# Attention with a routed expert layer on one core: half of a block's second layer in the next expert's code, the hint first, and h transposed ahead of layer 1

## The chip, the cores and the metric

The kernel runs on 1 core of one Trainium2 chip. The metric is device time in microseconds (us). Before the change three runs gave 288.33, 290.68 and 290.84 us, the median is 290.68 us.

## The reference

The reference computes causal attention (2 batches, 8 heads, 576 positions, head size 64) mixed with a memory read-out, and sends its 1152 rows of 512 numbers through a layer of 8 experts. A row goes to the expert with the largest gate logit. An expert keeps at most 288 rows.

```python
logits = x @ w_gate;  expert_idx = np.argmax(logits, axis=1)      # 8 experts
disp[e, counts[e]] = x[i]                                         # rows of an expert, in order
h = np.maximum(np.einsum('ecd,edf->ecf', disp, w1), 0.0)          # layer 1: 512 -> 1024
y = np.einsum('ecf,efd->ecd', h, w2)                              # layer 2: 1024 -> 512
out[i] = gate_w[i] * y[expert_idx[i], pos[i]]
```

With the inputs used the experts are wanted by 12, 149, 0, 58, 1, 558, 9 and 365 rows.

## The kernel before

The first half of the kernel (attention, gate, routing) is laid out by a planner, the class `Steps`: each step has costs and due times, and the planner writes the instructions in the order in which its model runs them. It also hands out buffers of each kind, such as the softmax buffers "p". The second half is written in a fixed order, and it is where the change lies.

An expert's rows are cut into a first block of 32 rows, and up to two further blocks of 128. The count of further blocks, `cr[e]`, is 0, 1 or 2; here it is 0, 1, 0, 1, 0, 2, 0, 2 for the experts 0 to 7. It is read from memory into registers at run time (`counts_in`), and TensorE, VectorE, ScalarE and GpSimd branch on it.

The loop at line 1117 writes one stretch of code for each expert e. In order:

- a branch hint for TensorE (line 1118), which names the branch `rest{e}` and carries whether `cr[e] > 0`;
- `first_g1(e + 1)` (L799): layer 1 of the next expert's first block, and its relu to h on ScalarE (L800). For expert 0 it stands ahead of the loop, and so ahead of the hint;
- `first_turn(e)`: two transposes of h (L805), copied to hT by VectorE (L806);
- `first_g2(e)` (L814): layer 2 of the first block from hT, a scaling on VectorE (L816), and a scatter to the output on GpSimd (L753);
- `rest(e)`: a branch (L917) on `cr[e] > 0`, and inside it one branch for exactly one further block (`one`, L918) and one for two (`two`, L921). Where `cr[e]` is 0 the engines jump over both;
- `more_rows(e + 2)` (L715): GpSimd gathers the rows of the further blocks of expert e + 2;
- `paced(e + 4)` (L689, L703): SyncE loads the weights of expert e + 4.

`one` transposes the gathered rows (L749), copies them by ScalarE (L846), runs layer 1 (L851), splits h and the weights w2 into a rounded part and its rest (`split`, L824 on ScalarE and L825 on VectorE; four buffers of each in rotation), and runs layer 2 as 8 x 3 matmuls into one bank (L858). `put` scales the result (L833) and scatters it. `two` does the same for 256 rows with all of layer 1 split (L887), and layer 2 as 8 x 3 x 2 matmuls (L895), of which those with the rests are issued as two halves of 256 columns. Its block 1 is complete first, and block 2 still has its last 12 matmuls to do behind that.

Ahead of the loop stand, for the last two token tiles, `late_rows` (L771), which adds their rows to the first blocks by a selection matmul. The first blocks lie in two groups of four experts, g = 0 and 1; `upright(g)` (L761, L763) transposes what was gathered early, and `first_x(g)` copies the result for layer 1.

## Time and profile before

| | us |
|---|---|
| median of three runs | 290.68 |
| the profiled execution's own time | 289.64 |
| its span, first to last instruction | 287.9 |
| TensorE busy | 250.7 (87% of the span) |
| VectorE, ScalarE, GpSimd busy | 175.2, 138.2, 71.5 |

The span is time between the first and last instruction of the program; 1.74 us of the execution's time lie around it. A busy share is a mean over stages: up to about 142 us the attention runs, from there to the end the experts. A row of the list in order of time gives start, length, engine, line, operation, and in brackets the idle time of the engine just before it with what ended that. PEq and DVEq stand for the sequencers of TensorE and VectorE, at branches above all.

### The profile page before, as it was taken

How to read it: one execution, taken by the hardware profiler on the slowest of the kernel's cores; microseconds unless marked ns; L12 is line 12 of the kernel's file. 1: busy time of each engine (PE TensorE's matmuls, PEld its weight loads, DVE VectorE, ACT ScalarE, POOL GpSimd, SP SyncE). 2: the span in 40 equal slices, each digit the busy share in tenths (PEclk: the TensorE clock that was granted, in tenths of full speed). 3: DMA queues.
4: the chain of work that ended last, by engine and by line, in shares of the span. 5: the costliest groups of instructions: out<-in, count | busy, mean ns of one | idle time of the engine just before them, and what ended most of it. 6: DMA issues, size and time to landing. Idle time of an engine off the chain costs nothing.

```text
span 287.9 us, 6958 instructions
## 1 busy us (share of the span) xinstructions
PE 250.7 (87%) x2545; PEld 201.4 (70%) x2545; DVE 175.2 (61%) x461; ACT 138.2 (48%) x400; POOL 71.5 (25%) x87
## 2 busy tenths in 40 slices
PE   8989998989879999999993798489977999769992
PEld 6676776677667678878862496358745999549991
DVE  2998899976999989768520136112713873138731
ACT  4779876886867787640310134004403652026520
POOL 2413274352573502223011100301051000520002
PEclk9999999999999999999999899979999999999999
DMA  6969887969899499352246773868688770410001
GB/s 193 387 213 341 286 300 221 369 264 323 282 296 323 115 283 374 96 237 79 86 142 197 237 227 137 278 235 255 209 245 275 225 219 6 120 48 0 2 0 74
DMA packets 23955, 58.97 MB, mean 205 GB/s; under 512 B 2636, under 2 KB 9296, under 8 KB 23906
## 3 DMA queue, kind: packets, MB, share of 16 engines
q1 hardware_dynamic: 22530, 54.60, 57.0%
q0 software_dynamic: 1376, 3.75, 4.0%
q8 instruction: 27, 0.44, 0.6%
q14 instruction: 22, 0.18, 0.2%
HBM read 51.96 MB, written 6.82 MB: 204 GB/s over the span
## 4 chain that ended last, share of the span: by engine, by line
DMA 37%; issue 22%; PE 22%; DVE 11%; POOL 4%; ACT 2%; POOLq 1%; SPq 0%; ACTq 0%; DVEq 0%
DMA xe<-x_scr,igf 16%; DMA out<-ys,isc 9%; PE ps L344 5%; DMA q<-qk 4%; DMA out<-yo,isc 4%; PE ps L365 3%; DMA xg<-x_scr,ig 3%; PE ps L380 2%; PE ps L332 2%; PE ps L333 2%; PE ps L469 2%; PE ps L405 2%; PE ps L477 2%; DMA w<-qk 1%; DVE phi L974 1%
## 5 line engine op out<-in xcount | busy, mean ns | idle before, releaser
L340 ACT ACTIVATE p<-ps,nmx 128x128 f32<-128x128 f32 (+3 forms) x64 | 33.8, 533 | 7.0 <-DVE nmx L337 6.0
L825 DVE TENSOR_TENSOR lr<-w,hr 128x512 fp32r<-128x512 f32 x40 | 26.7, 689 | 6.8 <-ACT hr L824 4.8
L337 DVE TENSOR_REDUCE nmx<-ps 128x1 f32<-128x128 f32 (+3 forms) x64 | 29.3, 479 | 1.6 <-PE ps L334 0.7
L344 PE MATMUL ps<-cs,p 128*128 128x128 f32 x160 | 28.4, 285 | 1.4 <-ACT pT L252 0.9
L824 ACT CAST hr<-w 128x512 fp32r<-128x512 f32 x40 | 23.9, 618 | 9.0 <-PE ps L895 5.4
L252 ACT COPY pT<-ps 128x256 f32<-128x256 f32 (+4 forms) x62 | 24.1, 414 | 5.0 <-PE ps L344 2.5
L800 ACT ACTIVATE h<-ps 128x256 f32<-128x256 f32 x8 | 3.1, 383 | 48.2 <-PE ps L799 36.5
L753 POOL DMA_INDIRECT out<-yo,isc x6 | 5.9, 982 | 76.9 <-DVE yo L833 49.1
L799 PE MATMUL ps<-w,xf 128*32 128x256 f32 x192 | 14.1, 446 | 9.4 <-PEq L917 8.6
L814 PE MATMUL ps<-w,hT 128*32 128x128 f32 x512 | 16.7, 274 | 5.7 <-DVE hT L806 5.0
L344 PEld LDWEIGHTS ps<-cs,p 128*128 128x128 f32 x160 | 17.6, 141 | 5.6 <-ACT p L340 1.7
L365 PE MATMUL ps<-pT,v 128*64 128x256 f32 (+1 forms) x144 | 20.6, 352 | 0.0
L814 PEld LDWEIGHTS ps<-w,hT 128*32 128x32 f32 x512 | 13.8, 110 | 8.5 <-DVE hT L806 7.1
L806 DVE COPY hT<-ps 128x256 f32<-128x256 f32 x8 | 3.4, 425 | 26.3 <-PE ps L805 26.3
L829 DVE SCALAR_TENSOR_TENSOR hl<-ps,hh 128x256 fp32r<-128x256 f32 (+1 forms) x20 | 9.5, 477 | 15.8 <-ACT hh L828 15.7
L457 DVE TENSOR_TENSOR x<-ps,tmp 128x288 f32<-128x288 f32 (+2 forms) x37 | 16.0, 442 | 2.4 <-PE ps L477 2.0
L828 ACT ACTIVATE hh<-ps 128x256 fp32r<-128x256 f32 (+1 forms) x20 | 8.5, 426 | 18.4 <-PE ps L851 9.7
L753 POOL DMA_INDIRECT out<-ys,isc x8 | 8.0, 1002 | 37.0 <-DVE ys L816 26.4
L533 POOL TENSOR_TENSOR xr<-x 128x512 f32<-128x512 f32 (+1 forms) x8 | 10.3, 1284 | 27.4 <-DVE x L457 14.9
L799 PEld LDWEIGHTS ps<-w,xf 128*32 128x32 f32 x192 | 6.7, 125 | 14.8 <-issue 12.7
L279 POOL TENSOR_SCALAR q<-q 64x640 f32<-64x640 f32 (+1 forms) x14 | 11.7, 848 | 20.7 <-DMA q<-qk 20.4
L365 PEld LDWEIGHTS ps<-pT,v 128*64 128x64 f32 x144 | 12.3, 136 | 5.5 <-issue 0.7
(203 smaller groups left out, 665.8 us busy)
## 6 DMA issues: line engine op xcount, KB each, us to landing
w<-w SPq DMA_DIRECT2D x56, 512.0 KB
w0s<-w SPq DMA_DIRECT2D x8, 512.0 KB
q<-qk SPq DMA_DIRECT2D x7, 576.0 KB
kt<-qk SPq DMA_DIRECT2D x7, 576.0 KB
v<-v SPq DMA_DIRECT2D x8, 320.0 KB
phi<-qp SPq DMA_DIRECT2D x8, 288.0 KB
out<-zer SPq DMA_DIRECT2D x4, 576.0 KB
x_scr<-xr SPq DMA_DIRECT2D x8, 256.5 KB
```

The lines of the kernel that those rows point to most:

```text
L252: nc.scalar.copy(out=o, in_=i_)
L279: en(e).tensor_scalar(out=i_[64:128], in0=i_[64:128], scalar1=SCALE, scalar2=1.0, op0=ALU.mult, op1=ALU.mult)
L337: nc.vector.tensor_reduce(out=nm[:, j:j + 1], in_=Z[Sk][:, :w], axis=AX.X, op=ALU.max, negate=True)
L340: nc.scalar.activation(out=Z[pk][:, :w], in_=Z[Sk][:, :w], func=AF.Exp, bias=nm[:, j:j + 1], accum_out=sums[:, t, 2 * p + j:2 * p + j + 1])
L344: nc.tensor.transpose(Z[Tk][:, 128 * kb:128 * kb + 128], Z[pk][:, 128 * kb:128 * kb + 128], ident)
L365: nc.tensor.matmul(Z[M][64 * j:64 * j + 64, c:128 * mg], vt[n % 2][:, kb, 64 * j:64 * j + 64], Z["pT", n, gi, j][:, 128 * mg * kb + c:128 ...
L457: nc.vector.tensor_tensor(out=xa[:R, a:c, :], in0=m()[:, :, 0:LC], in1=bc(r, R, c - a, LC), op=ALU.mult)
L753: s = nc.gpsimd.indirect_dma_start(out=out if k else out0, out_offset=bass.IndirectOffsetOnAxis(ap=isc[:, cc:cc + 1], axis=0), in_=yo, in_ ...
L799: nc.tensor.matmul(ps[g * W0:(g + 1) * W0, 0:FG], xT[:, c, e * W0:(e + 1) * W0], a[:, c, g * FG:(g + 1) * FG], start=(c == 0), stop=(c == 3))
L814: nc.tensor.matmul(ps[y * W0:(y + 1) * W0, 0:DG], hT[:, 128 * r + g * W0:128 * r + (g + 1) * W0], c2[:, g * nr + r, y * DG:(y + 1) * DG], ...
L824: nc.scalar.copy(out=hv, in_=wv)
L825: return hv, lv, lambda: nc.vector.tensor_tensor(out=lv, in0=wv, in1=hv.bitcast(F32), op=ALU.subtract)
```

## The change

- `one` stops after the first 12 of its 24 layer 2 matmuls. The other 12 and `put` become a function `last(e)`, which stands in the next expert's stretch, right behind its hint, under a condition of its own. `two` does all of block 2 first and the first 12 matmuls of block 1, and leaves the other 12 of block 1 to `last(e)`. For expert 7 `last` stays inside `rest`.
- Some matmuls are issued as two halves of 256 columns, by a count for each expert (`FILL`), which sets how many instructions a stretch has. The warm-up at the start has 50 matmuls of 152 columns in place of 30 of 256.
- In each stretch `first_turn(e)` stands ahead of `first_g1(e + 1)`. In expert 0's stretch the hint stands ahead of `first_g1(1)`, and `upright(1)`, `late_rows(1)` and `first_x(1)` follow `first_turn(0)`.
- `more_rows(e + 2)` moves into the next stretch, behind `last(e)`.
- In `one`, the copy of the transposed rows is shared between ScalarE and VectorE.
- The buffers that `late_rows` reads (one "p" buffer, now fixed for this use, and the two "xr") move to the pool that stays open to the end; the counts are read ahead of `first_g1(0)`.

```diff
-HALF = 8
+FILL = ((34, 0), (34, 8), (34, 8), (34, 8), (34, 8), (34, 8), (34, 8), (0, 0))
...
+                for k in self.fixed.keys() & st[x][4] - self.at.keys():
+                    t0 = max([t0, *(b[0] for b in self.kinds[k[0]] if b[1] == self.fixed[k])] if any(b[1] == self.fixed[k] for b in self.kinds[k[0]]) else [float("inf")])
...
-    Z.buffers("p", [ap.tile([128, 512], F32, name=f"p{x}") for x in range(P["np"])])
+    Z.buffers("p", [(ap if x < P["np"] - 1 else const).tile([128, 512], F32, name=f"p{x}") for x in range(P["np"])])
+    Z.fixed["p", "pick"] = P["np"] - 1
...
-    Z.buffers("xr", [ap.tile([128, XW], F32, name=f"xr{x}") for x in range(2)])
+    Z.buffers("xr", [const.tile([128, XW], F32, name=f"xr{x}") for x in range(2)])
...
         x_t(e, 1, mps[3])
-        nc.scalar.copy(out=xT.rearrange("p c r -> p (c r)"), in_=mps[3])
+        i_ = mps[3].rearrange("p (c r) -> p c r", c=4)
+        nc.scalar.copy(out=xT[:, 0:2], in_=i_[:, 0:2])
+        nc.vector.tensor_copy(xT[:, 2:4], i_[:, 2:4])
...
-        for f in range(8):
+        for f in range(4):
             for y, (u, v) in enumerate(((hh, 0), (hl, 0), (hh, 1))):
-                nc.tensor.matmul(mps[2], u[:, f, 0:128], w[f][v], start=(f == 0 and y == 0), stop=(f == 7 and y == 2))
+                n = 2 if 3 * f + y > 11 - FILL[e][1] else 1
+                for z in range(n):
+                    c = slice(DM // n * z, DM // n * (z + 1))
+                    nc.tensor.matmul(mps[2][:, c], u[:, f, 0:128], w[f][v][:, c], start=(f == 0 and y == 0), stop=False)
             take()
+
+    def last(e):
+
+        hh, hl = mt_["hh"], mt_["hl"]
+        for f in range(4, 8):
+            hv, lv = mt_["hr"][f % 4], mt_["lr"][f % 4]
+            for y, (u, v) in enumerate(((hh, hv), (hl, hv), (hh, lv))):
+                nc.tensor.matmul(mps[2], u[:, f, 0:128], v, start=False, stop=(f == 7 and y == 2))
         put(e, 1, mps[2])
...
+        left = [FILL[e][0]]
+
         def g2(f, k):
...
-                n = 2 if f < HALF and i else 1
+                n = 2 if (f or i) and left[0] > 0 else 1
+                left[0] -= n - 1
...
-            g2(f, 1)
+            g2(f, 2)
             if f < 4:
-                g2(f, 2)
-        put(e, 1, mps[2])
-        for f in range(4, 8):
-            g2(f, 2)
+                g2(f, 1)
         put(e, 2, mps[3])
...
             with tc.If(cr[e] > 1, label=f"two{e}"):
                 two(e)
+            if e == E - 1:
+                last(e)
...
-        Z.add({"P": (213 * P["wu"][0], 0, 13, 107)}, lambda e: warm(P["wu"][0] + 8), ["zer"], [], -9e9)
+        Z.add({"P": (213 * P["wu"][0], 0, 13, 107)}, lambda e: warm(P["wu"][0] + 28, 152), ["zer"], [], -9e9)
...
         late_rows(0)
-        for g in range(1, NF):
-            upright(g)
-            late_rows(g)
         late_probs(fps)
...
-        for g in range(NF):
-            first_x(g)
+        first_x(0)
+        cr.extend(counts_in(ET.PE, ET.DVE, ET.Activation, ET.Pool))
         first_g1(0)
...
-        first_g1(1)
-        cr.extend(counts_in(ET.PE, ET.DVE, ET.Activation, ET.Pool))
         for e in range(E):
             tc.mark_branch_hint_location(f"rest{e}", hint=cr[e] > 0, engines=[ET.PE])
-            if 1 <= e < E - 1:
+            if e == 0:
+                first_g1(1)
+            else:
+                with tc.If(cr[e - 1] > 0):
+                    last(e - 1)
+                if e - 1 + LK < E:
+                    more_tiles(e - 1 + LK)
+                    more_rows(e - 1 + LK)
+            first_turn(e)
+            if e == 0:
+                for g in range(1, NF):
+                    upright(g)
+                    late_rows(g)
+                    first_x(g)
+            elif e < E - 1:
                 first_g1(e + 1)
-            first_turn(e)
             first_g2(e)
             rest(e)
-            if e + LK < E:
-                more_tiles(e + LK)
-                more_rows(e + LK)
             if e + 4 < E:
                 paced(e + 4)
```

## Rows read from the trace of the kernel before

**Rows 1.** The page's first part: busy time, share of the span, instructions.

```profile
PE 250.7 (87%) x2545; PEld 201.4 (70%) x2545; DVE 175.2 (61%) x461; ACT 138.2 (48%) x400; POOL 71.5 (25%) x87
```

**Rows 2.** TensorE in order of time: expert stretches 1 to 7.

```profile
157.70 3.31 PE L799 MATMUL ps<-w,xf 128*32 128x256 f32 x32 [4.34 <-PEq L917]
...
187.31 3.19 PE L799 MATMUL ps<-w,xf 128*32 128x256 f32 x32 [3.46 <-PEq L917]
...
208.84 1.93 PE L799 MATMUL ps<-w,xf 128*32 128x256 f32 x32 [0.73 <-PEq L921]
...
211.66 1.84 PE L814 MATMUL ps<-w,hT 128*32 128x128 f32 x49 [0.52 <-DVE hT L806]
213.82 0.68 PE L814 MATMUL ps<-w,hT 128*32 128x128 f32 x15 [0.33 <-issue]
215.36 1.93 PE L799 MATMUL ps<-w,xf 128*32 128x256 f32 x32 [0.85 <-PEq L917]
...
218.18 1.96 PE L814 MATMUL ps<-w,hT 128*32 128x128 f32 x64 [0.52 <-DVE hT L806]
...
249.80 1.39 PE L814 MATMUL ps<-w,hT 128*32 128x128 f32 x38 [1.42 <-DVE hT L806]
251.53 1.05 PE L814 MATMUL ps<-w,hT 128*32 128x128 f32 x26 [0.34 <-issue]
253.05 0.43 PE L805 MATMUL ps<-cs,h 128*128 128x128 f32 x2 [0.47 <-PEq L917]
```

**Rows 3.** Stretches: us, busy (instructions) by engine, granted clock, DMA share, GB/s.

```profile
157.70:163.80 6.10, 5.58 (x98) 3.32 (x98) 0.42 (x1) 0.38 (x1) 0.00 (x0) 0.77 0.64 201
...
187.30:193.70 6.40, 5.76 (x98) 3.38 (x98) 0.47 (x2) 0.38 (x1) 0.00 (x0) 0.73 0.71 238
208.20:214.60 6.40, 4.83 (x98) 3.00 (x98) 1.17 (x3) 0.38 (x1) 3.04 (x3) 1.00 0.82 228
```

**Rows 4.** TensorE in order of time: expert 1's single block.

```profile
164.10 0.63 PE L749 MATMUL ps<-cs,xg 128*128 128x128 f32 x4 [0.25 <-issue]
165.44 7.41 PE L851 MATMUL ps<-x,w 128*128 128x128 f32 x64 [0.72 <-ACT x L846]
172.61 0.47 PE L858 MATMUL ps<-hr,hh 128*128 128x512 f32 x1
...
177.95 0.39 PE L858 MATMUL ps<-lr,hh 128*128 128x512 f32 x1
179.08 1.93 PE L799 MATMUL ps<-w0s,xf 128*32 128x256 f32 x32 [0.74 <-PEq L921]
```

**Rows 5.** In order of time, TensorE and VectorE: the second group's late rows.

```profile
142.37 0.39 PE L761 MATMUL ps<-zer 128*128 128x512 bf16 x1
...
145.55 1.31 PE L777 MATMUL ps<-xr,p 128*128 128x1 f32 x8
...
142.87 0.42 DVE L783 COPY xf<-ps 128x256 f32<-128x256 f32 x1 [2.26 <-ACT xf L782]
```

**Rows 6.** GpSimd and TensorE in order of time; last row: gathered tile's landings.

```profile
212.33 1.02 POOL L715 DMA_INDIRECT xg<-x_scr,ig  x1 [0.31 <-issue]
...
249.86 1.02 POOL L715 DMA_INDIRECT xg<-x_scr,ig  x1 [0.31 <-issue]
...
220.92 1.07 PE L749 MATMUL ps<-cs,xg 128*128 128x128 f32 x8 [0.79 <-DVEq L918]
...
257.03 1.09 PE L749 MATMUL ps<-cs,xg 128*128 128x128 f32 x8 [1.08 <-DVEq L918]
...
DMA to landing us min/median/max: 6.0/6.1/6.3
```

**Rows 7.** TensorE in order of time: layer 2 of expert 5's two blocks.

```profile
234.61 0.40 PE L895 MATMUL ps<-hr,hh 128*128 128x512 f32 x1
...
245.75 0.40 PE L895 MATMUL ps<-lr,hh 128*128 128x256 f32 x2
```

**Rows 8.** SyncE's queue in order of time: expert 6's first weights, fourth piece landed.

```profile
206.71 0.24 SPq L703 DMA_DIRECT2D seen<-w  x1
```

More of the change, by code (lines that the diff above doesn't have):

```diff
@@ L48, in __init__ @@
         self.steps, self.writer, self.readers, self.kinds, self.at = [], {}, {}, {}, {}
+        self.fixed = {}
     def buffers(self, kind, tiles):
@@ L118, in emit @@
                 if k not in self.at:
-                    b = min(self.kinds[k[0]])
+                    b = min(b for b in self.kinds[k[0]] if b[1] == self.fixed.get(k, b[1]))
                     self.kinds[k[0]].remove(b)
@@ L891, in g2 @@
             for i, (a, v) in enumerate(((hh, hv), (hl, hv), (hh, lv))):
-                n = 2 if f < HALF and i else 1
+                n = 2 if (f or i) and left[0] > 0 else 1
+                left[0] -= n - 1
                 for y in range(n):
                     c = slice(DM // n * y, DM // n * (y + 1))
-                    nc.tensor.matmul(mps[1 + k][:, c], a[:, f, 128 * k - 128:128 * k], v[:, c], start=(f == 0 and i == 0), stop=(f == 7 and i == 2 and y == n - 1))
+                    nc.tensor.matmul(mps[1 + k][:, c], a[:, f, 128 * k - 128:128 * k], v[:, c], start=(f == 0 and i == 0), stop=(k == 2 and f == 7 and i == 2 and y == n - 1))
         for f in range(2):
```

## Prediction

> **What bounds the kernel now.** I read the first part of the page first: TensorE is busy 87% of the span, no other engine over 61% [rows 1]. So what TensorE does not do in the expert part is what can be won, and I went through that part in TensorE's order of time and wrote down every idle time. Three kinds recur. The first is the jump over an expert without further blocks, put down to TensorE's own sequencer: 4.34 us ahead of stretch 1, 3.46 ahead of 3, but only 0.85 ahead of 5 and 0.47 ahead of 7 [rows 2]. The second stands behind the transposes of h in every stretch: 0.52 us until VectorE has copied hT, 1.42 in stretch 6 [rows 2]. The third is 0.73 or 0.74 us behind a single block [rows 2, 4]. The table by stretches adds that the two long jumps cost twice: in the stretch behind them the granted clock is 0.77 and 0.73, elsewhere 1.00 [rows 3], and the first layer 1 there takes 3.31 and 3.19 us in place of 1.93 [rows 2]. [...] Idle times of 0.85 and 1.42 us lowered nothing that shows.
>
> Why two jumps are cheap and two dear: the hint stands at the head of a stretch (for expert 0 behind its layer 1), so I took the time from there to the jump. In stretch 4 it is 5.67 us (208.84 to 215.36 less 0.85), in 2 it is 4.77 (179.08 to 187.31 less 3.46), in 6 about 6.5 (from 246.1, where the last row of layer 2 ends, to 253.05 less 0.47) [rows 2, 4, 7]. In 0 it is about 2.9, worked out as the 5.67 less its layer 1 (1.93) and less 0.88, by which its layer 2 is longer than the usual 1.96 (211.66 to 214.50, with a pause of 0.33) [rows 2]. From hint to the next work that makes 7.2, 8.2, 6.5 and 7.0 us. **I read it so:** what the hint starts takes 5.7 us or more, and the jump waits for what is left. In both stretches with a cheap jump layer 2 has that pause and takes 0.82 to 0.88 us more (stretch 6: 249.80 to 252.58); I count it as a price of a hint that takes effect.
>
> **The change part by part.** All against the profiled execution, 289.64 us.
>
> The jumps. In stretches 2, 4 and 6 the change puts the last 12 matmuls of the block between hint and jump. Layer 2 of a single block goes at 0.232 us per matmul (172.61 to 177.95, 23 steps) [rows 4], so that is 2.8 us, and with transposes and layer 1 (208.84 to 211.66 less 0.52: 2.30) and layer 2 (1.96) the hint has 7.1 us [rows 2]. In stretch 0 it has layer 1 (1.93), the transposes (0.4), the second group's late rows (142.37 to 145.55, 3.18 us [rows 5]) and layer 2: 7.4. Both exceed the 5.67 that sufficed, so I take all jumps at 0.47 (bounds 0.47 and 0.85).
>
> The added condition. Where the expert before had no further block it is another short jump: bounds 0.13 (a condition that falls through, below) and 0.47 (the whole cheapest jump); I take 0.47 as the nearest, since that too is a jump with TensorE drained. Where `last` runs, the condition falls through: two such ahead of L749 take 0.25 us together [rows 4], one 0.13; bounds 0 and 0.25; I take 0.14. Behind two blocks (245.75, next work at once) it is covered by queued matmuls, of which 2.8 us are left; uncovered it would be 0.14. An engine queued behind the condition: GpSimd waits in it for `put` before it gathers for expert e + 2, as it did before; VectorE has to scale `put` (0.75) ahead of copying hT, and layer 1 of 1.9 us covers both.
>
> So, gap by gap (idle before to idle after, other terms): stretch 0 to 1: 4.34 to 0.94, 3.40 won, 0.85 lost to the pause, 1.38 won on the clock (3.31 to 1.93) = 3.93. Stretch 2 to 3: 3.46 to 0.94, 2.52 won, 0.85 lost, 1.26 won = 2.93. Stretch 4 to 5: 0.85 to 0.94, 0.09 lost.
>
> hT. With layer 1 (1.93) between transposes and layer 2, the 0.52 is covered in stretches 0 to 5 (in 0 by the late rows), 6 x 0.52 = 3.12. If that cover were gone it would cost just this. Stretch 7 has no layer 1 left and keeps it.
>
> The single blocks: the shared copy turns a wait of 0.72 into about 0.56, half of the copy against VectorE's 0.42 for 256 columns [rows 4, 5], 0.16 won; the condition costs 0.14; twice, 0.04 together. The 8 halves cost 0.005 each (0.2370 a matmul with halves, 234.61 to 245.75 in 47 steps, against 0.232 [rows 4, 7]), nothing.
>
> At nothing: the late rows of group 1 move behind the hint, 3.18 us go and come back; the copy of group 0 for layer 1 ends at 143.29 [rows 5], while `late_probs` of 1.25 us keeps TensorE busy from 142.37 to 143.6. Without that cover it would cost 0.9. The warm-up has 7600 columns for 7680; 20 more matmuls at 0.005 are 0.1. The counts are read while late rows are queued.
>
> **Sum up to expert 5's blocks:** 3.93 + 2.93 - 0.09 + 3.12 + 0.04 = 9.93, TensorE would be there at 220.92 - 9.93 = 210.99.
>
> What is late next: the gathers, which follow the block two experts earlier. Block 3 ended at 208.84 - 0.73 = 208.11, the second gather for expert 5 was issued at 212.33, took 1.02 and landed 6.1 later [rows 2, 6]: 219.45, 11.34 behind. GpSimd's steps to it stay. Block 3 now ends at 208.84 - 9.93 + 0.52 + 0.52 - 0.09 = 199.86, so the rows are there at 211.20: 0.21 lost, 9.72 stay. For expert 7 the gather of 249.86 landed at 256.98 and the transposes began at 257.03 [rows 6]: they waited for it, not for TensorE. That path hangs on the end of expert 5, 246.15, and stays at 10.9 us, TensorE needing about 9.8. So what stretch 6 gains (1.42) is lost in this wait. Expert 7's layer 2 without halves: 48 x 0.005 = 0.23 won. The tail behind it is the same.
>
> Weights: the fourth piece of expert 6's first weights was there by 206.71 [rows 8], needed at 215.36 less 9.4 = 206.0. Their loads wait for the buffers of experts 0, 1 and 2, which come free 4 us earlier and more, so 0.7 at worst, none taken.
>
> Total won 9.95: 279.7 against the profiled 289.64. That execution lies 1.04 under the median and 1.31 over the lowest run; I add half of the 1.04: **280.2**. Bounds of this case: without the pauses and with the added jump at 0.13, 2.4 less, and gathers 0.5 to 1 sooner, twice: 276; with jumps at 0.85, conditions at 0.25 and the second gather 1 us later, 2.5 more: 283.
>
> **Rivals.** *One dear jump stays.* It is not the time but the place: hints at the head of stretch 2 and in the middle of stretch 0 failed, others held, and the new places may serve only one. Then 3.9 or 2.9 come back: 283 to 284. The regular order by time speaks against it; that stretch 2's hint missed with 4.77 us where 5.67 sufficed speaks for it. A gather of 1.5 us more at three experts gives the same. 0.20.
>
> *The hints do nothing, both dear jumps stay,* and the change does not do what it says. Then 3.12 + 0.04 - 0.09 + 0.23 less 2 x 0.47 for the added jumps is 2.4 won: 287.3 against the profiled execution, 287.8 with half of the 1.04. That 0.85 and 0.47 stand at jumps over the same two blocks as 4.34 and 3.46 speaks against it: something shortens them. 0.12. [...]
>
> *Slower: the two cheap jumps become dear.* The stretches are longer or shorter by the moved matmuls and `FILL`; if the code that each hint fetches now ends short of the jump's target, stretches 4 and 6 miss as 0 and 2 do. On top of 287.8: stretch 4's gap 0.94 to 4.37, the clock 1.3, the pause 0.88 back = 3.9; stretch 6 the same less the 1.1 of slack against the gather = 2.8: 294.5. It decides from the point where a jump's target lies outside what was fetched, in every stretch at once. For it: the costs at the jumps differ by 3.9 us, so a little decides. Against: the count is the same in every stretch, so the change can be even. 0.08.
>
> **The numbers.** My forecast 0.60, one dear jump or slow gathers 0.20, no effect 0.12, slower 0.08. The range from 275.8 to 287.5 holds the first two whole and the edge of the third, a little over 0.8; the first alone has 276 to 283. A change under 1% (2.9 us) can't be told from none here; 287.8 is that limit. Faster 0.82 (the first two and little of the third), within 0.10, slower 0.08.
>
> **What would show it.** Right: in TensorE's order of time no idle over 1.5 us ahead of stretches 1 and 3, granted clock 1.00 in both, no wait for hT but in stretch 7, and 0.8 to 1.0 us behind a single block's first half. Gathers: expert 7's transposes about 11 us behind expert 5's end. Wrong: 3 us or more at any of the four jumps; layer 1 slowed; a stretch's jump over `last` longer than 0.5.

## The result and the profile after

The changed kernel takes 276.17 us (median of 4 runs, 274.85 to 277.69), the kernel before on the same chip 290.76 us (288.33 to 291.54): ratio 0.951, 95% interval 0.944 to 0.959. Some executions are slower, at a lower granted clock (of a_turn, 295.45 us at 0.958 where the fastest takes 287.14 at 0.992); all ratios and intervals of this document leave them out and so need not be the ratio of the two medians. The forecast was 280.2 us, in a range of 275.8 to 287.5. The direction, the range and the forecast case held (its own bounds were 276 to 283); the gain is 4 us larger than the sum.

The profiled execution took 276.45 us with a span of 274.7 us, 13.2 us less than before. The page's busy line and the granted clock in its 40 slices:

```profile
PE 246.4 (90%) x2551; PEld 202.0 (74%) x2551; DVE 175.8 (64%) x463; ACT 137.6 (50%) x400; POOL 71.5 (26%) x87
...
PEclk9999999997999999999999999999999999999998
```

TensorE's share rises from 87% to 90%, and in the expert part only the last slice, in which TensorE is nearly idle, shows a lowered clock (0.8). TensorE in order of time, the rows that answer to [rows 2, 4] (start, length, engine, line; in brackets the idle time ahead and what ended it):

```profile
155.66 0.41 PE L809 MATMUL ps<-cs,h 128*128 128x128 f32 x2 [1.11 <-PEq L1136]
...
159.91 0.63 PE L753 MATMUL ps<-cs,xg 128*128 128x128 f32 x4 [0.22 <-issue]
161.04 7.42 PE L857 MATMUL ps<-x,w 128*128 128x128 f32 x64 [0.51 <-ACT x L851]
...
172.67 0.47 PE L876 MATMUL ps<-hr,hh 128*128 128x512 f32 x1 [1.38 <-DVEq L938]
...
175.52 0.38 PE L809 MATMUL ps<-cs,h 128*128 128x128 f32 x2
175.83 1.93 PE L803 MATMUL ps<-w0s,xf 128*32 128x256 f32 x32
177.58 1.93 PE L818 MATMUL ps<-w,hT 128*32 128x128 f32 x64
180.58 0.41 PE L809 MATMUL ps<-cs,h 128*128 128x128 f32 x2 [1.07 <-PEq L1136]
...
184.83 0.63 PE L753 MATMUL ps<-cs,xg 128*128 128x128 f32 x4 [0.23 <-issue]
...
200.41 0.38 PE L809 MATMUL ps<-cs,h 128*128 128x128 f32 x2
...
205.46 0.41 PE L809 MATMUL ps<-cs,h 128*128 128x128 f32 x2 [1.06 <-PEq L1136]
205.80 1.50 PE L803 MATMUL ps<-w,xf 128*32 128x256 f32 x24
207.61 0.64 PE L803 MATMUL ps<-w,xf 128*32 128x256 f32 x8 [0.31 <-DMA w<-w]
...
210.46 1.09 PE L753 MATMUL ps<-cs,xg 128*128 128x128 f32 x8 [0.46 <-PEq L935]
...
235.70 0.38 PE L809 MATMUL ps<-cs,h 128*128 128x128 f32 x2
...
240.74 0.41 PE L809 MATMUL ps<-cs,h 128*128 128x128 f32 x2 [1.05 <-PEq L1136]
241.66 1.96 PE L818 MATMUL ps<-w,hT 128*32 128x128 f32 x64 [0.52 <-DVE hT L810]
244.12 1.08 PE L753 MATMUL ps<-cs,xg 128*128 128x128 f32 x8 [0.50 <-PEq L935]
```

The four jumps stand at 1.05 to 1.11 us each, layer 1 behind them at 1.93 us. Between turn, layer 1 and layer 2 of a stretch (175.52 to 179.51) there is no idle time, and no wait for hT but in stretch 7. Layer 2 has no pause in any stretch. Behind a single block's first half stand 1.38 us, put down to VectorE. The stretches that answer to [rows 3] (us, busy by engine, granted clock):

```profile
155.70:159.90 4.20, 3.98 (x98) 2.88 (x99) 0.57 (x2) 0.38 (x1) 1.02 (x1) 1.00 0.78 248
180.60:184.80 4.20, 4.00 (x98) 2.87 (x99) 0.56 (x2) 0.39 (x1) 0.61 (x1) 1.00 0.72 217
```

Clock 1.00 in both, where it was 0.77 and 0.73.

To see where the time came from I measured the same intervals in both traces, from the start of the first late rows (142.18 now, 140.29 before) to the end of the span:

| interval | before | after | won | forecast |
|---|---|---|---|---|
| late rows to expert 1's block | 23.81 | 17.73 | 6.08 | 4.97 |
| expert 1's block to the next stretch's work | 14.98 | 15.61 | -0.63 | 0.02 |
| from there to expert 3's block | 14.79 | 9.31 | 5.48 | 3.97 |
| expert 3's block | 14.97 | 15.58 | -0.61 | 0.02 |
| from there to expert 5's blocks | 12.08 | 10.05 | 2.03 | 0.74 |
| expert 5's blocks with the last half | 25.16 | 25.24 | -0.08 | 0 |
| from there to expert 7's blocks | 10.95 | 8.42 | 2.53 | 0 |
| from there to the end | 30.87 | 30.58 | 0.29 | 0.23 |
| sum | 147.61 | 132.52 | 15.09 | 9.95 |

The part ahead of the late rows is 1.89 us longer in this execution. No step of the change accounts for that, and over the variants below the start of the late rows varies from 139.5 to 145.1 us, so I leave it open.

The traces also hold, though no view lists them, when TensorE's sequencer executed each hint and each branch, how long the branch took, and when each 16 KB fetch of TensorE's code began and landed (queue q8 of the page: 26 packets, 0.43 MB). For the four jumps, the time from the hint to the branch that jumps over `rest{e}`, and what that branch took:

| jump out of stretch | before: hint to branch, us | branch | after: hint to branch, us | branch |
|---|---|---|---|---|
| 0 | 2.73 | 4.47 | 7.22 | 0.41 |
| 2 | 4.23 | 3.56 | 6.97 | 0.36 |
| 4 | 5.37 | 0.76 | 6.90 | 0.36 |
| 6 | 7.84 | 0.36 | 7.07 | 0.36 |

One reading fits all 56 jumps of these four stretches in the 14 traces. In 38 the last fetch had landed 1.86 us or more ahead of the branch, which took 0.35 to 0.41 us. In the other 18 the branch took 0.76 to 5.25 us and ended 1.32 to 1.55 us behind the landing of a fetch. So a dear jump here waits for a fetch of code. In stretches 0 and 2 before, that fetch began only 1.46 and 1.22 us into the branch.

### The profile page after: what moved, and what is told of

Read it like the earlier page. It is cut to its first block, busy times and chain, and to the rows that moved or that the text cites. A ratio compares the mean times of both kernels' runs of the same rounds, so it can differ in the third digit from the quotient of the medians.

```text
span 274.7 us, 7067 instructions
## 1 busy us (share of the span) xinstructions
PE 246.4 (90%) x2551; PEld 202.0 (74%) x2551; DVE 175.8 (64%) x463; ACT 137.6 (50%) x400; POOL 71.5 (26%) x87
## 5 line engine op out<-in xcount | busy, mean ns | idle before, releaser
L820 DVE TENSOR_SCALAR ys<-ps,prb 128x128 f32<-128x128 f32 x8 | 2.8, 351 | 21.7 <-PE ps L818 21.7
L336 PE MATMUL ps<-k,qs 128*128 128x128 f32 (+3 forms) x40 | 16.2, 405 | 0.0
L818 PE MATMUL ps<-w,hT 128*32 128x128 f32 x512 | 15.5, 273 | 0.5 <-DVE hT L810 0.5
L338 PE MATMUL ps<-cb 128*128 128x128 bf16 x64 | 15.0, 235 | 0.0
L481 PE MATMUL ps<-iw_sb,oT 128*128 128x144 f32 (+1 forms) x80 | 13.5, 297 | 1.5 <-DVE x L461 1.5
```

The lines of the kernel that those rows point to most:

```text
L336: nc.tensor.matmul(ps[:, :w], lh, k1[:, j, :w], start=True, stop=False)
L338: nc.tensor.matmul(ps[:, q0:w], identb, maskb, start=False, stop=True)
L481: nc.tensor.matmul(ps[:R, 2 * LC * x:2 * LC * (x + 1)], oT[b * NP + p][:, q0:q0 + R], iw_sb[:, p, :], start=True, stop=True)
L818: nc.tensor.matmul(ps[y * W0:(y + 1) * W0, 0:DG], hT[:, 128 * r + g * W0:128 * r + (g + 1) * W0], c2[:, g * nr + r, y * DG:(y + 1) * DG], ...
```

## The experiments

Names with b_ are the kernel before with an edit, those with a_ the changed kernel with an edit. They ran on three chips (the first four, the next four and the last four share one), on which the kernel before took 292.85, 292.90 and 297.15 us. The unedited changed kernel was not run beside them, so the ratios to the kernel before are what can be compared, with care where the chips differ:

| run | us | ratio to before | 95% interval |
|---|---|---|---|
| b_shift2 | 292.76 | 0.989 | 0.978 to 1.000 |
| b_pad | 301.27 | 1.027 | 1.019 to 1.035 |
| a_shift6 | 288.18 | 0.982 | 0.975 to 0.990 |
| a_nolast | 283.18 | 0.969 | 0.960 to 0.978 |
| a_late6 | 285.33 | 0.972 | 0.955 to 0.990 |
| a_first6 | 286.92 | 0.988 | 0.981 to 0.995 |
| a_hintlate | 282.99 | 0.973 | 0.963 to 0.984 |
| a_turn | 290.21 | 0.996 | 0.989 to 1.002 |
| a_nohint | 304.59 | 1.040 | 1.011 to 1.068 |
| a_late2 | 281.98 | 0.961 | 0.950 to 0.973 |
| a_first40 | 287.56 | 0.973 | 0.940 to 1.005 |
| a_hintin | 281.92 | 0.963 | 0.944 to 0.981 |

The theory of the prediction was time: a hint works where about 5.7 us lie between it and the jump. Its rival was place: it depends on where hint or target stand in the code.

### b_shift2: all code of the kernel before two instructions earlier

```diff
-lambda e: warm(P["wu"][0] + 8)
+lambda e: warm(P["wu"][0] + 7)
```

> The kernel before with 29 warm-up matmuls in place of 30, so that all later code of TensorE lies two instructions earlier and nothing else differs. Place theory (a hint takes effect only if it lies near enough to the start of the block of code that TensorE fetches; stretch 2's hint lay two instructions too far): the idle ahead of stretch 3 falls from 3.46 to under 1 us and its layer 1 from 3.19 to 1.93, the other jumps as before, 286 to 288 us. Time theory (a hint takes effect if 5.7 us or more pass between it and the jump): no idle changes by over 0.5 us, 290 to 291 us.

TensorE in order of time, the rows ahead of stretches 1 and 3:

```profile
158.35 3.64 PE L799 MATMUL ps<-w,xf 128*32 128x256 f32 x32 [5.07 <-PEq L917]
...
190.28 3.31 PE L799 MATMUL ps<-w,xf 128*32 128x256 f32 x32 [3.71 <-PEq L917]
```

The hint of stretch 2, its jump and the jump's target all lie two instructions earlier, and the jump costs 3.71 us all the same (3.46 before [rows 2]). The place theory with its two instructions fails in stretch 2.

### b_pad: three matmuls between hint and jump in every stretch of the kernel before

```diff
-                n = 2 if f < HALF and i else 1
+                n = 2 if f < 6 and i or (f == 6 and i == 1) else 1
...
+            for x in range(3):
+                nc.tensor.matmul(mps[7], ident, wt[e, 0][:, x, 0:512], start=True, stop=True)
```

> The kernel before with three matmuls of 512 columns added to every stretch between hint and jump, whose result is not used, about 2.7 us, and six halves fewer in layer 2 of two blocks, so that every hint stays exactly where it was. Time theory: the idle ahead of stretch 3 falls from 3.46 to 0.5 to 0.9 us, ahead of 1 from 4.34 to 1 to 2 (its hint then has 5.6 us), with the clock at 1.00 in stretch 3. Place theory: 3.46 and 4.34 stay within 0.5 us. The added work itself costs about 8 x 2.7 us under either, so only the idle times tell.

```profile
159.76 1.94 PE L799 MATMUL ps<-w,xf 128*32 128x256 f32 x32 [3.21 <-PEq L917]
...
182.40 1.93 PE L799 MATMUL ps<-w0s,xf 128*32 128x256 f32 x32 [0.75 <-PEq L921]
184.26 2.84 PE L1122 MATMUL ps<-w,cs 128*128 128x512 f32 x6
...
190.30 1.93 PE L799 MATMUL ps<-w,xf 128*32 128x256 f32 x32 [0.51 <-PEq L917]
```

In stretch 2 the time from hint to jump rises from 4.77 to 7.39 us (182.40 to 190.30 less 0.51), and the jump falls from 3.46 to 0.51 us. Hint and target lie where they lay, so this is the run that speaks most plainly for time; the fetch now begins 3.12 us ahead of the branch. In stretches 0 and 4 it does not: in 0 the branch comes 5.33 us behind the hint and the jump still costs 3.21, with the fetch begun 0.98 us into the branch; in 4 there are 6.85 us for 5.37, and the jump is dearer than before, 1.38 us for 0.85. A fixed time that suffices does not exist here.

### a_shift6: all code of the changed kernel six instructions later

```diff
-lambda e: warm(P["wu"][0] + 28, 152)
+lambda e: warm(P["wu"][0] + 31, 144)
```

> The changed kernel with 53 warm-up matmuls of 144 columns in place of 50 of 152: all later code of TensorE lies six instructions later, nothing else differs. Place theory: the hints of all stretches lie as far from the start of a block as the one that failed before; the jumps ahead of stretches 1, 3, 5 and 7 cost 3.5 to 4.5 us and lower the clock behind them, 287 to 293 us. Time theory: as the changed kernel, jumps of 1.1 us, 275 to 278 us.

```profile
161.71 0.41 PE L809 MATMUL ps<-cs,h 128*128 128x128 f32 x2 [4.25 <-PEq L1136]
...
187.25 1.16 PE L818 MATMUL ps<-w,hT 128*32 128x128 f32 x33 [0.31 <-issue]
189.44 0.41 PE L809 MATMUL ps<-cs,h 128*128 128x128 f32 x2 [1.04 <-PEq L1136]
```

By the ratios (two chips) most of the gain is gone. The jump of expert 0 is dear again with the same work between hint and jump, and layer 1 behind it takes 3.54 us for 1.93 (at a clock of 0.77 it took 3.31 in the kernel before [rows 2, 3]); those of stretches 2, 4 and 6 stay at 1.04, 1.10 and 1.02 us. Pauses stand inside layer 2 of stretches 2, 4 and 6. Neither theory says this: time holds in three stretches, place in one.

### a_nolast: the second half back behind the first

```diff
-            if e == E - 1:
-                last(e)
+            last(e)
...
-                with tc.If(cr[e - 1] > 0):
-                    last(e - 1)
```

(With other counts in `FILL`, so that the hints keep their places within some 25 instructions.)

> The changed kernel with the last half of a block's layer 2 back inside the block's own branch, so that no expert has the added condition; the counts of halves are set so that every hint stays within one instruction of its place. Between hint and jump 4.0 us are left in stretches 2, 4 and 6, and 7.4 in stretch 0. Time theory: stretches 3 and 5 and 7 have 2 to 3.5 us of idle ahead of them, stretch 1 under 1; the added condition saves 0.6 at four jumps and 0.6 behind two single blocks: 279 to 284 us. Place theory: all four jumps cost 0.5 to 0.9 us, 271 to 274 us.

```profile
155.62 0.43 PE L809 MATMUL ps<-cs,h 128*128 128x128 f32 x2 [0.52 <-PEq L934]
...
172.68 0.47 PE L876 MATMUL ps<-hr,hh 128*128 128x512 f32 x1 [1.36 <-DVEq L938]
...
181.83 0.43 PE L809 MATMUL ps<-cs,h 128*128 128x128 f32 x2 [1.21 <-PEq L934]
...
210.31 0.43 PE L809 MATMUL ps<-cs,h 128*128 128x128 f32 x2 [2.15 <-PEq L934]
```

Expert 0's jump without a condition behind it costs 0.52 us, with one 1.11: the condition takes 0.59 of these (0.47 forecast). The gap ahead of `last` is there without any move into the next stretch, 1.36 us. The moved half earns little here: jumps of 1.21 and 2.15 us in place of 1.07 and 1.06, but 0.52 and 0.47 in place of 1.11 and 1.05 where the condition is saved, 4.35 in sum for 4.29. As a test of time this run, too, fails: TensorE's sequencer reached the hints early, and the branches of stretches 2 and 4 come 5.80 and 7.83 us behind them; that 7.83 us leave 2.15 of the jump speaks against time alone.

### a_late6: only the code behind expert 0's jump six instructions later

```diff
-FILL = ((34, 0), ...
+FILL = ((34, 3), ...
```

> The changed kernel with FILL[0] = (34, 3) in place of (34, 0): three more matmuls of expert 0's single block, which is jumped over, are written as halves, so that all code behind expert 0's jump lies six instructions later, while expert 0's own stretch and its hint lie where they lay. Moving everything by six (the run before) cost a jump of 4.25 us at expert 0, pauses inside layer 2 of stretches 2, 4 and 6, and 1.34 us where expert 5's block begins. Theory L (a hint is lost where it stands right behind the start of a fetched piece of code, and the pauses come from where the later code lies): the jump of expert 0 stays at 1.1 us with the clock up, the pauses return (stretch 2 +1.1, stretch 4 +2.6, stretch 6 +2.5, block of expert 5 +0.9): 276.2 + 7.1 = 283 us (281 to 285). Rival P (it is the place at which a jump lands that sets its cost): the jump of expert 0 costs 4.25 us and the clock falls, +5 us on top: 288 us. Rival T (only time between hint and jump counts, and the run before was dear for another reason): 276 us, no pauses.

```profile
158.00 0.41 PE L809 MATMUL ps<-cs,h 128*128 128x128 f32 x2 [1.12 <-PEq L1136]
...
181.20 0.44 PE L818 MATMUL ps<-w,hT 128*32 128x128 f32 x4 [0.20 <-issue]
```

Expert 0's jump stays at 1.12 us: where it lands is not what made it dear. The pauses are there, as theory L expected; the next run shows that its reason for them is wrong.

### a_first6: only expert 0's stretch six instructions later

```diff
-FILL = ((34, 0), ...
+FILL = ((31, 0), ...
...
-lambda e: warm(P["wu"][0] + 28, 152)
+lambda e: warm(P["wu"][0] + 31, 144)
```

> The counterpart: three more warm-up matmuls (53 of 144 columns) and FILL[0] = (31, 0), so that expert 0's hint and stretch lie six instructions later and everything behind its jump lies where the changed kernel has it. Theory L: the jump of expert 0 costs 4.25 us, layer 1 behind it runs at the low clock (3.54 for 1.93 us), together +4.9 us, and nothing else changes from expert 1 on: 281 us, or up to 284 if the 2.9 us that the run before lost ahead of the experts return too. Rivals P and T: expert 0's jump stays at 1.1 us, 276 to 279 us.

```profile
155.87 0.41 PE L809 MATMUL ps<-cs,h 128*128 128x128 f32 x2 [3.98 <-PEq L1136]
156.21 2.88 PE L803 MATMUL ps<-w,xf 128*32 128x256 f32 x32
```

The jump of expert 0 costs 3.98 us, although some 7.3 us lie between its hint and the jump as before (in this run from the start of the next expert's layer 1 at 144.60 to 151.89; from hint to branch 7.25, 7.22 in the changed kernel). So it is a place that counts here. Hint and jump both lie six instructions later, and this run does not part the two. The fetch tells what went wrong: it begins 0.93 us into the branch, as in a_nohint below (0.92), where in the changed kernel it has landed 4.3 us ahead. The pauses in stretches 2, 4 and 6 are there too (0.52, 1.34 and 1.33 us of idle inside layer 2), with all that code where the changed kernel has it: the place of the code does not explain them.

### a_first40: expert 0's stretch 40 instructions later

```diff
-FILL = ((34, 0), ...
+FILL = ((14, 0), ...
...
-lambda e: warm(P["wu"][0] + 28, 152)
+lambda e: warm(P["wu"][0] + 48, 109)
```

> As the run that moved expert 0's stretch by six instructions (a jump of 3.98 us), but by 40: 70 warm-up matmuls of 109 columns and FILL[0] = (14, 0), so that expert 0's hint stands 40 instructions behind its place in the changed kernel and all code behind its jump where it was. Theory L (a hint is lost where it stands right behind the start of a fetched piece of code): 40 instructions on, the hint is 1 us and more behind that start and works again: jump 1.1 us, clock up, 276 us, or 283 with the pauses that both six-instruction runs showed. Rival B (expert 0's hint works only ahead of the boundary): jump about 4 us and a slow layer 1, 281 us, or 287 with the pauses.

```profile
158.12 0.66 PE L809 MATMUL ps<-cs,h 128*128 128x128 f32 x2 [3.15 <-PEq L1136]
```

Theory L falls (40 instructions on, the hint does not work again); rival B holds: the jump stays dear and layer 1 behind it takes 3.64 us; where its boundary lies, no run shows. Over all runs expert 0's jump costs, by the place of its hint, in instructions behind the changed kernel's:

| place of expert 0's hint | jump ahead of stretch 1, us |
|---|---|
| 0 | 1.11, a_late6 1.12, a_late2 1.05, a_hintlate 1.06, a_turn 1.05, a_hintin 1.22, a_nolast 0.52 |
| 6 | a_shift6 4.25, a_first6 3.98 |
| 40 | a_first40 3.15 |
| that of the kernel before, in b_shift2 two earlier | b_shift2 5.07, before 4.34, b_pad 3.21 |
| no hint | a_nohint 3.50 |

At the first of these places the hint works; at the others it does little or no better than no hint (in the kernel before and its two variants there was also less time, 2.7 to 5.3 us from hint to branch). Why, the runs don't show. It is no rule for the other stretches: moved by the same six instructions in a_shift6, the hints of stretches 2, 4 and 6 work (1.04, 1.10 and 1.02 us), and in stretch 2 the same place goes with a jump of 3.46 us in the kernel before and of 0.51 in b_pad.

### a_nohint: no hint for any rest branch

```diff
-            tc.mark_branch_hint_location(f"rest{e}", hint=cr[e] > 0, engines=[ET.PE])
```

(`FILL` by one count more or less, so that the jumps land where they did.)

> The changed kernel without the hints of the rest branches (the hint inside rest stays; FILL holds the places at which the jumps land within one instruction). Theory T of the prediction (a hint's fetch has to be under way for some us before the jump): without it all four jumps cost 3.5 to 4.3 us, less the 0.3 that the hint's own two instructions take behind a jump, and layer 1 behind three of them runs 1.3 to 1.6 us longer at the low clock; the gap behind a single block falls from 1.38 to 1.08: 276.2 + 4 x 2.7 + 3 x 1.4 - 0.6 = 290 us (287 to 293). Rival N (hints do nothing, only the layout does): jumps 0.75 us, 274 us. For the pauses inside layer 2 that four of the variants show in stretches 2, 4 and 6: if they belong to the fetch that a hint starts, none is seen here.

```profile
158.71 0.41 PE L809 MATMUL ps<-cs,h 128*128 128x128 f32 x2 [3.50 <-PEq L1135]
...
181.91 0.42 PE L818 MATMUL ps<-w,hT 128*32 128x128 f32 x4 [0.21 <-issue]
...
188.16 0.66 PE L809 MATMUL ps<-cs,h 128*128 128x128 f32 x2 [4.32 <-PEq L1135]
...
220.90 0.66 PE L809 MATMUL ps<-cs,h 128*128 128x128 f32 x2 [4.85 <-PEq L1135]
...
263.46 0.66 PE L809 MATMUL ps<-cs,h 128*128 128x128 f32 x2 [4.11 <-PEq L1135]
```

The stretch behind the second of them (columns as above; the clock is the third number from the right):

```profile
188.20:193.80 5.60, 5.37 (x98) 3.32 (x99) 0.57 (x2) 0.38 (x1) 0.00 (x0) 0.74 0.60 195
```

All four jumps cost 3.5 to 4.85 us, and behind the last three the clock is down (0.74, 0.66 and 0.50): the rival that hints do nothing falls. The run is 4% slower than the kernel before, and above the expected 287 to 293 us; the pauses were not in that sum, the rest is open. In each of the four jumps a fetch begins 0.9 to 2.0 us into the branch, which ends 1.3 to 1.5 us behind its landing. The pauses inside layer 2 are there without hints, so they are no price of a hint, as the prediction had it.

### a_hintlate: the hint behind last(e)

```diff
-            tc.mark_branch_hint_location(f"rest{e}", hint=cr[e] > 0, engines=[ET.PE])
             if e == 0:
+                tc.mark_branch_hint_location(f"rest{e}", hint=cr[e] > 0, engines=[ET.PE])
                 first_g1(1)
             else:
                 with tc.If(cr[e - 1] > 0):
                     last(e - 1)
+                tc.mark_branch_hint_location(f"rest{e}", hint=cr[e] > 0, engines=[ET.PE])
```

> The changed kernel with the hint behind last(e) in place of ahead of it in every stretch but the first (FILL holds the places at which the jumps land within one instruction). From hint to jump it is then some 4.4 us in stretches 2, 4 and 6, where it was 7.6 us. Theory of time: the jumps cost about 3.5 us (a jump 4.9 us behind its hint cost 3.46 in the kernel before), and layer 1 behind them runs 1.26 us longer at the low clock: up to 2.4 + 1.3 in each of three, less 0.3 for the hint no longer issued in the gap behind a single block: 284 to 287 us. Theory L alone or P: the jumps stay at 1.0 us, 275.5 to 276.5 us.

```profile
181.19 0.43 PE L809 MATMUL ps<-cs,h 128*128 128x128 f32 x2 [1.18 <-PEq L1136]
```

Jumps of 1.18, 1.11 and 1.11 us, and the pauses. As a test of time the run fails: TensorE's sequencer runs ahead of the queued matmuls and reached the hint at 172.31, only 0.6 us behind the first matmul of `last`, so that 6.91 us remain to the branch, for 6.97 in the changed kernel.

### a_turn: the transposes of h behind layer 1 again

```diff
-            first_turn(e)
             if e == 0:
...
             elif e < E - 1:
                 first_g1(e + 1)
+            first_turn(e)
             first_g2(e)
```

> The changed kernel with first_turn(e) behind first_g1(e + 1) as before, the rest unchanged. By the sum of the prediction: 0.52 us of waiting for hT returns in six stretches and the first one, 3.1 to 3.6 us: 279.6 us (279.2 to 280.2). Rival: the sequencer works on through the waits and the jumps' 1.05 us get shorter by as much where a jump follows, so that about half of it is given back: 278 us.

```profile
181.14 1.95 PE L818 MATMUL ps<-w,hT 128*32 128x128 f32 x64 [1.47 <-issue]
...
209.32 2.09 PE L818 MATMUL ps<-w,hT 128*32 128x128 f32 x64 [2.20 <-issue]
```

The wait for hT is 0.88 us in stretch 0 and 0.52 in 1, 3 and 5; in stretches 2, 4 and 6 stand 1.47, 2.20 and 2.19 us where a_late6 on the same chip has pauses of 0.52, 1.21 and 1.32 us inside layer 2. That is 0.88 + 1.56 + 0.95 + 0.99 + 0.87 = 5.25 us of idle added, and in and behind stretch 6 layer 2 itself takes 2.97 and 3.21 us for the 1.95 of stretch 2. Against a_hintlate (ratio 0.973) the run stands at 0.996. On this chip, with the pauses that all variants have, the early transposes are worth more than the 3.1 to 3.6 expected, and nearly all of the gain. What they are worth without pauses was not run.

### a_late2: the code behind expert 0's jump two instructions later

```diff
-FILL = ((34, 0), ...
+FILL = ((34, 1), ...
```

> The changed kernel with FILL[0] = (34, 1): the code behind expert 0's jump lies two instructions later (six cost pauses of 6 us in sum, 281 to 285 us). If the place alone decides on the pauses, two instructions are on one side or the other: 276 us without, or some 283 us with pauses in stretches 2, 4 and 6; if they come and go with the timing of the fetches, stretches differ and the time lies between.

```profile
179.90 0.44 PE L818 MATMUL ps<-w,hT 128*32 128x128 f32 x4 [0.19 <-issue]
```

The pauses stand in all three stretches. From the start of `last` to the end of the jump it is 9.25 us in stretch 2 and 10.60 in 4, in the changed kernel's profile 7.91 and 7.89; from expert 5's blocks to the end of the jump of stretch 6 31.00 for 28.31. Together 6.7 us; between the two medians, of different chips, lie 5.8 (281.98 and 276.17).

### a_hintin: a try at a faster version

```diff
+        if e < E - 1:
+            tc.mark_branch_hint_location(f"rest{e + 1}", hint=cr[e + 1] > 0, engines=[ET.PE])
         for f in range(4):
             for y, (u, v) in enumerate(((hh, 0), (hl, 0), (hh, 1))):
...
+            if f == 4 and e < E - 1:
+                tc.mark_branch_hint_location(f"rest{e + 1}", hint=cr[e + 1] > 0, engines=[ET.PE])
             g2(f, 2)
```

> A try at a faster version. The hint for rest{e + 1} moves out of the stretch's start into one(e) (behind its layer 1) and two(e) (its layer 2, at f = 4); expert 0's stays where it is, and FILL holds the places at which the jumps land within one instruction. The two instructions of the hint (0.3 us) are then no longer issued in the gap behind a single block nor behind a jump: 0.3 us in two gaps and behind four jumps, 1.8 us: 274.4 us, jumps of 0.75 us, gaps of 1.08 us; from hint to jump it is then over 10 us in stretches 2, 4 and 6. Rival: code fetched between hint and jump (the end of one, the next stretch) pushes the hinted code out, and the jumps of stretches 2 and 4 cost 3.5 to 4.3 us with the clock down behind them, 276 + 8 = 284 us; or the pauses appear, 281 us.

TensorE, and then VectorE, in order of time:

```profile
171.84 0.47 PE L878 MATMUL ps<-hr,hh 128*128 128x512 f32 x1 [1.38 <-DVEq L942]
...
180.69 0.41 PE L809 MATMUL ps<-cs,h 128*128 128x128 f32 x2 [0.80 <-PEq L1140]
```

```profile
168.92 2.69 DVE L829 TENSOR_TENSOR lr<-w,hr 128x512 fp32r<-128x512 f32 x4
```

The hints work from inside the block (0.80, 0.86 and 0.87 us, about 0.2 less each), but the gap ahead of `last` stays at 1.38, expert 0's jump is 1.22, and the pauses are there. The ratio is 0.963, on another chip and with a wide interval, against 0.951 for the change as made: that it is faster is not shown.

## Why the prediction was right, and where it was wrong

**The jumps.** Forecast 0.94 us each with the condition, measured 1.05 to 1.11; the dear jumps and the low clock behind them (0.77 and 0.73 [rows 3], now 1.00) are gone, which is the core of the gain, and a_nohint shows that the hints do it. The condition was under-sized (0.59 for 0.47), over the 0.5 that the prediction itself had named as a sign of being wrong.

**The reason for them** was half right. That a jump waits for what is left holds: for a fetch, and 1.32 to 1.55 us behind its landing. The times read from the rows were close for stretches 0, 2 and 4 (2.9, 4.77 and 5.67 for 2.73, 4.23 and 5.37) and too short for 6 (6.5 for 7.84). In stretch 2 time decides: 4.77 us and 3.46 in the kernel before, 7.39 us and 0.51 in b_pad with hint and target at the same place. But a time that suffices everywhere there is not: in a_first6 the fetch that expert 0's jump waits for had not begun 7.25 us behind the hint, when the branch came, and in a_nolast's stretch 4 it began 7.7 us behind the hint. For expert 0 the step "Both exceed the 5.67 that sufficed" gave the right number on a wrong ground, and there the number is luck: 7.3 us did not suffice in a_first6, and what helped is where the new layout happens to put expert 0's stretch. The rival "one dear jump stays" had the mechanism, a place that serves or not; a_shift6 loses 4.75 us there (3.14 at the jump, 1.61 in layer 1) for the 3.9 that it priced, and the pauses on top.

**The pause** was forecast to come in stretches 0 and 2 and to stay in 4, 0.85 each. It stands in none, which is 2.55 us that the sum took off in vain, and its explanation was wrong: a_nohint has pauses in stretches without a hint. In the kernel before, the two stretches with a cheap jump were also the two in which GpSimd issues two gathers beside layer 2 (212.33 and 249.86 [rows 6] are the second ones), so those rows could not tell a hint's price from a gather's.

**hT**: 0.52 covered in six stretches, as forecast. The sum left out that with h turned early the transposes, layer 1 and layer 2 also run into each other: 2.06 us from the transposes' start to layer 2's (175.52 to 177.58) for 2.30 without the wait before. That is 0.24 in stretches 2 and 4, 0.2 in 0, 1 and 3, and nothing in 5, where 2.61 less the wait of 0.31 is 2.30 again; 1.1 us in sum.

**The single blocks** failed: 0.02 won each was forecast, 0.6 is lost. The copy came out as said (0.51 for a forecast of 0.56), but the gap ahead of `last` is 1.38 and 1.35 us for 0.88 (its bounds were 0.8 to 1.0). VectorE in order of time shows what it waits for:

```profile
169.74 2.70 DVE L829 TENSOR_TENSOR lr<-w,hr 128x512 fp32r<-128x512 f32 x4
```

VectorE's splits end at 172.44, and TensorE starts at 172.67, 0.23 behind; in a_hintin 171.61 and 171.84, 0.23 again. So I read it: the first matmul of `last` waits, across the end of the branch, until VectorE has passed it too (it signals at 172.51, and TensorE's wait for that signal ends at 172.62), and VectorE passes it only behind its last split, whose result the last matmul alone needs. I had read the gap from TensorE's own sequencer [rows 4] and missed that the cut puts a branch's end between a split and its reader. That is also why a_hintin won nothing there.

**The gathers.** For expert 5 a loss of 0.21 was forecast, none is seen. For expert 7 the step "they waited for it, not for TensorE" failed: I added the landing time to the end of the issue, but it counts from the issue. GpSimd, the landings of the gathered tile, and TensorE's weight loads now:

```profile
239.56 1.01 POOL L719 DMA_INDIRECT xg<-x_scr,ig  x1 [0.31 <-DMA out<-yo,isc]
```

```profile
DMA to landing us min/median/max: 4.5/5.3/6.1
```

```profile
244.11 0.85 PEld L753 LDWEIGHTS ps<-cs,xg 128*128 128x128 f32 x8 [0.76 <-DMA xg<-x_scr,ig]
```

The rows are used 4.55 us behind the start of the issue, which only the landing time so counted allows. Before, the gather of 249.86 had then landed at 255.96 [rows 6], as TensorE finished layer 2, and the wait of 1.08 was the one that the row names, for VectorE's branch; in b_pad it is 1.08 again, although the gather there, issued at 258.69, had long landed when the transposes began at 269.82. So stretch 6's gain was not lost: 2.53 us for 0. Now the gather ends this wait, with nothing to spare.

**The weights** of expert 6 were costed at nothing; TensorE now waits 0.31 us for them inside layer 1 of stretch 5 (207.61 in the list above).

**Two small terms** that the sum left out won 0.3 each. Ahead of expert 5's blocks the wait at the branch fell from 0.79 to 0.46 us. And the low clock before (0.73 [rows 3]) had slowed stretch 3's transposes too, which now take 0.41; TensorE before:

```profile
190.43 0.69 PE L805 MATMUL ps<-cs,h 128*128 128x128 f32 x2
```

Of the 5.14 us by which the expert part beats the sum: pauses 2.55, overlaps 1.1, expert 7's path 2.5, expert 5's gather 0.2, the two small terms 0.6, less 1.3 at the single blocks, 0.4 at three jumps and 0.3 for the weights, makes 4.95; 0.2 is unassigned.

**What stays open** is why every variant has pauses in layer 2 of stretches 2, 4 and 6 (a_turn has the idle time ahead of it), 6 to 7 us in all, and the profiled changed kernel none. In a_late6 layer 2 takes 3.2, 4.6 and 4.6 us there for 1.93. The pauses come with the code moved by 0, 2 or 6 instructions, with the hint early, late or absent. In the kernel before no fetch of TensorE's code is under way in the two pauses: the last ones had landed at 213.40 and 249.03, and the pauses begin at 213.50 and 251.19. What lies beside them in all variants are the gathers, as beside the pauses of the kernel before; GpSimd in order of time, a_late6:

```profile
246.09 1.05 POOL L719 DMA_INDIRECT xg<-x_scr,ig  x1 [0.30 <-issue]
247.45 1.02 POOL L719 DMA_INDIRECT xg<-x_scr,ig  x1 [0.31 <-DMA out<-yo,isc]
```

The four pauses of its stretch 6 lie between 246.57 and 249.15. With one gather, in stretch 2, there are one or two pauses, with two there are three or four. In b_pad, where the gathers are issued ahead of layer 2, it has none. But the changed kernel's own profile has its gathers beside layer 2 as well (202.92 to 205.30, layer 2 from 202.47 to 204.40) and no pause. So the gathers alone don't decide; whether the rest is a matter of small shifts or of the chip (the changed kernel was not run on those three) was not tried. Against the chip speaks that b_shift2, on another one, has the pauses of the kernel before, 0.28 and 0.32 us for 0.33 and 0.34. With the pauses a_late2 still stands at 0.961: that much of the gain does not hang on their absence.

## What to carry to other kernels

In this kernel a taken jump without a hint cost 3.50 to 4.85 us (a_nohint), behind three of the four with a granted clock of 0.50 to 0.74; with a hint it cost 0.5 to 1.2, but only where the last fetch of code had landed well ahead of the branch, 1.86 us or more. When that fetch begins could not be foretold from time or place alone, so read the cost at each jump again after every change in code length. When a sequence is cut at a branch's end, look at which engines feed the second part: here it started only when the slowest of them had passed the branch, 0.23 us behind VectorE's last split. And before counting a wait as a transfer's, check from where the view counts the landing.

## What the runs showed that I had not expected

A shift of six instructions seems to move the time by about 3% (a_shift6 0.982, against 0.951 on another chip), with the same instructions executed but for the warm-up. On one chip a_first6 and a_late6 stand at 0.988 and 0.972, with intervals that overlap a little; what is certain are the 3 us at expert 0's jump (3.98 for 1.12).

Inside layer 2 TensorE stood idle in the variants for 0.2 to 0.45 us at a time, waiting for nothing that the profile shows, two to five matmuls apart, with 26 to 39 of the 64 matmuls still to do. Nothing in the profile of the kernel before showed more than one such pause in a stretch [rows 2].
